# Issuing the first weight load and the x load in front of the program's opening all-engine barrier

## The chip, the cores and the metric

The kernel runs on one core of a Trainium2 chip, with nothing on the other cores. The metric is the device time of one execution in microseconds (us), as the median of several runs. A profile of one execution goes with each kernel; its "span" runs from the first to the last instruction of the program and is some 1.2 us shorter than the device time.

## The reference, cut to what matters

One decode step of two branches that share a layer norm of `x` (1024 values): attention over a cache of 65536 positions, and a small mixer with an MLP.

```python
xn = layernorm(x)                                    # 1 x 1024
q  = xn @ wq                                         # wq 1024 x 4096: 8.4 MB
o  = softmax(q k^T / sqrt(128)) v                    # k_cache, v_cache: 4 x 65536 x 128 each, 67 MB each
A  = o @ wo                                          # wo 4096 x 1024: 8.4 MB
B  = mixer and MLP of layernorm(xn) with w1, w2 (2.1 MB each), w3, w4 (7.3 MB each)
out = x + A + B
```

All is in bf16. There is one row of activations, so every weight and every cache element is read once and used little: about 170 MB go through the core for one row of output.

## The kernel before

The program is written engine by engine. Each engine has a list of operations and waits; at the end the lists are emitted. An engine's DMA issue is an ordinary entry in its list: the transfers of the weights and of the cache are issued by SP (SyncE), the load of `x` by ScalarE.

```python
def _dma(q, chan, fn, reads=(), writes=(), partial=False):
    _deps(q, reads, writes)              # waits for the buffer's readers and writers
    chan.n += 1
    ev = q.dma(fn, chan.sem, 16 * chan.n)
    ...
# the first loads: x on ScalarE's queue, 4 MB + 4 MB of wq and the first K and V blocks (4 MB each) on SP's
_dma(q_act, chan("x"), lambda e: e.dma_start(out=x_bf[:, :], in_=A_x[0, 0, :].rearrange("(p j) -> p j", p=P)), writes=[b_x])
load_rows(Kn[:, 1, :], b_K[1], "wqa", A_wq, 0, 4)
load_rows(Vn[:, 1, :], b_V[1], "wqb", A_wq, 4, 4)
...
issue_k(0)
issue_v(0)
# GpSimd: 12 memsets and 11 selects that build constants, then waits
...
# layer norm of x (DVE, PE, POOL), projection of q in two halves (wqa, then wqb), then
issue_k(1)                               # the buffer of wqa is free again
issue_v(1)                               # the buffer of wqb is free again
# 32 steps, 2 per K/V block; K and V have two buffers each; weights of the other branch go in between
...
q_sp.emit(nc.sync); q_act.emit(nc.scalar); q_pool.emit(nc.gpsimd); q_dve.emit(nc.vector); q_pe.emit(nc.tensor)
...
nc = _bacc.Bacc("TRN2", ...)             # this line (L653) emits a preamble: four constants written by
                                         # GpSimd, then a barrier of all engines, before anything above
```

The barrier of the preamble works so: every other engine executes a drain that counts up one semaphore; GpSimd runs a drain of its own, waits for the full count, then counts up a second semaphore that the others wait for. The semaphores named in the trace records of these instructions show this.

Of the kernel before, what the change touches and what calls it, by code (L numbers as in the profile page):

```python
# [123 lines left out]
def bass_parallel_sum__gqa_block_cached__mixer_s_mlp__decode_kernel(  # L124
# [30 lines left out]
    with ExitStack() as es:  # L155
# [476 lines left out]
        ev_out = _dma(q_sp, chan("out"), lambda e: e.dma_start(out=out[0, 0, :].rearrange("(j n) -> j n", j=4), in_=orow[0:97:32, :]), reads=[b_orow])  # L632
        q_sp.wait(ev_out)

        q_sp.emit(nc.sync)
        q_act.emit(nc.scalar)
        q_pool.emit(nc.gpsimd)
        q_dve.emit(nc.vector)
        q_pe.emit(nc.tensor)
# [28 lines left out]
```

## Time and profile before

The kernel before takes 403.08 us (403.03 to 403.28, 4 runs), with a span of 401.7 us.

| what | value | where to read it |
|---|---|---|
| busy share of VectorE, the busiest compute engine | 57% | first part of the page |
| mean busy share of the 16 DMA engines from 30 to 390 us | 1.00, at 432 GB/s | busy time by stretches |
| first load issued | 0.79 us | timeline |
| first packet of it starts | 1.83 us | packet records of the trace |
| last compute | 399.50 + 0.42 us | timeline |

These are lines of the page of the kernel before: busy time by engine, the rates in 40 slices, and the chain that ended last.

```profile
PE 186.4 (46%) x1859; PEld 78.5 (20%) x1875; DVE 228.4 (57%) x401; ACT 48.9 (12%) x128; POOL 61.8 (15%) x90
...
DMA  8999999999999999999999999999999999999994
GB/s 359 424 418 438 445 418 424 460 419 421 436 447 419 429 435 435 422 436 445 420 428 450 426 419 441 441 419 428 434 439 421 447 432 424 426 425 436 437 416 207
...
DMA 55%; DVE 24%; PE 16%; issue 2%; ACT 1%; SPq 0%; another core or an unknown queue 0%; POOL 0%; ACTq 0%
```

The busy time by stretches of the same kernel; the last two columns are the mean busy share of the DMA engines and what they moved.

```profile
30.00:390.00 360.00, 173.14 (x1664) 72.01 (x1680) 220.52 (x365) 47.03 (x126) 55.91 (x62) 0.55 1.00 432
390.00:402.00 12.00, 5.65 (x112) 2.91 (x112) 0.42 (x1) 0.00 (x0) 0.00 (x0) 0.64 0.54 228
```

The reader is to see two things. First, no compute engine is near its limit, while the DMA row is full in every slice but the first and the last. Second, the chain puts only 55% on the transfers and 24% on VectorE, which looks like a mixed bound. It is not one. A link of the chain such as "VectorE frees the K buffer, then the load of the next K block" begins at the issue of that load; but at its issue the queue still holds earlier loads. The page gives 27.3 us from issue to landing (the median of 15) for a K block of 4 MB that needs about 10 us of the stream by itself (4.19 MB at 432 GB/s). The packet records say it directly: between 2.75 and 395.1 us 15 to 19 data packets are in flight, 16.02 on average, which is one for each DMA engine.

So the run is a sum of three terms: the start of the stream (1.8 us to the first packet), 170.2 MB at 432 GB/s (394 us), and a tail, which is the remaining 5.9 us of the span. The change works on the first term. Here are lines of the timeline of the opening, and the last cast (start in us, duration in us, engine, line, operation).

```profile
0.79 0.40 ACTq L275 DMA_DIRECT2D x_bf<-in_A_x_dram  x1
...
0.79 0.40 SPq L272 DMA_DIRECT2D Kn<-in_A_wq_dram  x1
...
1.25 0.41 SPq L272 DMA_DIRECT2D Vn<-in_A_wq_dram  x1
...
13.05 0.17 DVE L326 CAST xT<-x_bf 128x8 f32<-128x8 bf16 x1 [11.60 <-DMA x_bf<-in_A_x_dram]
...
17.88 0.62 PE L376 MATMUL PT_ps<-Kn,xn_bf 128*32 128x512 bf16 x4
...
21.42 0.33 SPq L286 DMA_DIRECT2D Kn<-in_A_k_cache_dram  x1
...
399.50 0.42 DVE L631 CAST orow<-OUT_ps 128x256 bf16<-128x256 f32 x1 [12.73 <-PE OUT_ps L404]
```

And these are GpSimd's two steps of the barrier and the preamble's drains, from the view of the line that emits them (count, duration in ns, first and last start in us).

```profile
L653 POOLq EVENT_SEMAPHORE  x2: 17/17/17, 0.6 to 0.7; - x2
L653 SPq DRAIN  x1: 7/7/7, 0.0 to 0.0; - x1
...
L653 ACTq DRAIN  x1: 8/8/8, 0.1 to 0.1; - x1
...
L653 POOLq DRAIN  x1: 172/172/172, 0.4 to 0.4; - x1
```

SP is there at 0.00 us and has nothing to do until the barrier lets it go at 0.71. GpSimd's constants and drain hold the barrier: it begins to collect at 0.59. So the first load is issued only at 0.79 us, and its first packet starts at 1.83 us, although it needs nothing that the barrier protects.

The timeline also shows a second candidate for a gain: `x` is 2 KB and yet the first use waits for it until 13.05 us. Its 128 packets of 16 bytes sit between packets of 32 KB. The Trainium skill ("DMA: Bandwidth & Descriptors", section "Queues, rings and completion order") says that each DMA engine takes turns between its queues a packet at a time. The packet records agree: 16 packets of `x` start per round, as many as there are DMA engines, the first of them at 3.63, 4.84, 6.06 ... 12.14 us, 1.21 us apart, which is the duration of a 32 KB packet. An earlier `x` would start the layer norm and the projection earlier.

### The profile page before, as it was taken

The numbers are of one execution on the slowest core, as the hardware profiler recorded it, in microseconds if no ns is written. First come the engines' busy times: TensorE is split into PE (matmuls) and PEld (weight loads), VectorE is DVE, ScalarE is ACT, GpSimd is POOL, SyncE is SP. The second block draws the span as 40 slices with busy tenths as digits, with TensorE's granted clock in tenths as the row PEclk, the third lists the DMA queues.
The fourth block names the chain that finished last, engine by engine and source line by source line (L and its number), as shares of the span: only waits on it lengthen the run. The fifth ranks groups of instructions, "written<-read, shape, count | busy, mean of one in ns | idle before, by whom it ended". The sixth has DMA issues, their size and how long they took to land.

```text
span 401.7 us, 4776 instructions
## 1 busy us (share of the span) xinstructions
PE 186.4 (46%) x1859; PEld 78.5 (20%) x1875; DVE 228.4 (57%) x401; ACT 48.9 (12%) x128; POOL 61.8 (15%) x90
## 2 busy tenths in 40 slices
PE   0332325064525745285531965353433654444664
PEld 0211101021103511062110731121111311111132
DVE  0247566277816578255744287576836775788410
ACT  1000111011101011011110011111201111112100
POOL 5000003012211011110310101111110112112110
PEclk9985556556565556555655555656555656565566
DMA  8999999999999999999999999999999999999994
GB/s 359 424 418 438 445 418 424 460 419 421 436 447 419 429 435 435 422 436 445 420 428 450 426 419 441 441 419 428 434 439 421 447 432 424 426 425 436 437 416 207
DMA packets 7087, 170.19 MB, mean 424 GB/s; under 512 B 916, under 2 KB 920, under 8 KB 1048
## 3 DMA queue, kind: packets, MB, share of 16 engines
q1 hardware_dynamic: 6920, 169.87, 98.4%
q8 instruction: 15, 0.25, 0.2%
q14 instruction: 8, 0.07, 0.0%
q10 hardware_dynamic: 144, 0.00, 0.0%
HBM read 169.87 MB, written 0.00 MB: 423 GB/s over the span
## 4 chain that ended last, share of the span: by engine, by line
DMA 55%; DVE 24%; PE 16%; issue 2%; ACT 1%; SPq 0%; another core or an unknown queue 0%; POOL 0%; ACTq 0%
DMA Kn<-in_A_k_cache_dram 44%; DVE X L476 13%; DMA Kn<-in_B_w_dram 6%; DMA Vn<-in_A_wq_dram 5%; PE H_ps L366 4%; PE S_ps L488 3%; DVE pT_f L529 3%; PE OT_ps L536 3%; DVE mrow L495 3%; PE M_ps L366 1%; ACT p_sb L518 1%; PE PT_ps L527 1%; PE M_ps L564 1%; PE OUT_ps L404 1%; DVE Yall L393 1%
## 5 line engine op out<-in xcount | busy, mean ns | idle before, releaser
L476 DVE STREAM_TRANSPOSE X<-Kn 128x1024 f32<-128x1024 f32 x128 | 151.7, 1215 | 67.4 <-DMA Kn<-in_A_k_cache_dram 67.4
L536 PE MATMUL OT_ps<-Vn,pT_f 128*32 128x512 bf16 x512 | 60.7, 627 | 52.4 <-DVE pT_f L529 52.4
L488 PE MATMUL S_ps<-X,Yall 128*32 128x512 bf16 x512 | 59.1, 608 | 16.1 <-DVE X L476 16.1
L501 PE MATMUL MB_ps<-Rm,Lmat 128*128 128x16 bf16 x32 | 6.1, 192 | 90.1 <-DVE Rm L496 90.1
L550 POOL TENSOR_TENSOR O_acc<-O_acc,tmpO 128x513 f32<-128x513 f32 x28 | 32.8, 1172 | 88.6 <-ACT tmpO L544 88.6
L518 ACT ACTIVATE p_sb<-S_ps,brun 128x512 bf16<-128x512 f32 x32 | 22.0, 687 | 192.7 <-DVE brun L516 157.3
L548 POOL TENSOR_SCALAR O_acc<-O_acc,ff 128x513 f32<-128x513 f32 x28 | 19.5, 698 | 153.4 <-ACT ff L523 153.4
L495 DVE TENSOR_REDUCE mrow<-S_ps 128x1 f32<-128x512 f32 x32 | 21.6, 674 | 25.5 <-PE S_ps L488 25.5
L544 ACT ACTIVATE tmpO<-OT_ps 128x512 f32<-128x512 f32 x32 | 19.1, 598 | 108.0 <-PE OT_ps L536 108.0
L488 PEld LDWEIGHTS S_ps<-X,Yall 128*32 128x32 bf16 x512 | 16.6, 126 | 54.7 <-DVE X L476 38.2
L529 DVE STREAM_TRANSPOSE pT_f<-PT_ps 128x512 f32<-128x512 f32 x32 | 22.9, 716 | 6.1 <-PE PT_ps L527 4.2
L536 PEld LDWEIGHTS OT_ps<-Vn,pT_f 128*32 128x32 bf16 x512 | 14.6, 129 | 59.2 <-DVE pT_f L529 42.0
L501 PEld LDWEIGHTS MB_ps<-Rm,Lmat 128*128 128x128 bf16 x32 | 3.3, 102 | 114.9 <-DVE Rm L496 114.9
L527 PE MATMUL PT_ps<-p_sb,permR 128*128 128x512 bf16 x16 | 9.3, 580 | 21.4 <-ACT p_sb L518 21.4
L366 PEld LDWEIGHTS H_ps<-xn_bf,W 128*128 128x128 bf16 x224 | 14.4, 169 | 1.7 <-issue 1.7
L366 PE MATMUL H_ps<-xn_bf,W 128*128 128x1 bf16 x224 | 14.5, 202 | 0.0
L527 PEld LDWEIGHTS PT_ps<-p_sb,permR 128*128 128x128 bf16 x32 | 3.4, 105 | 41.4 <-ACT p_sb L518 41.4
L505 DVE TENSOR_REDUCE Bst<-MB_ps 128x1 f32<-128x16 f32 x32 | 5.6, 174 | 8.3 <-PE MB_ps L501 8.3
L330 PE MATMUL M_ps<-ln_s,ones_f 128*128 128x1 f32 x6 | 1.8, 362 | 17.3 <-DVE ln_s L329 17.3
L546 POOL COPY O_acc<-tmpO 128x513 f32<-128x513 f32 x4 | 2.4, 612 | 47.4 <-ACT tmpO L544 47.4
L404 PE MATMUL OUT_ps<-Kn,gh_bf 128*1 128x256 bf16 x112 | 5.6, 364 | 5.0 <-DMA Kn<-in_B_w_dram 5.0
L631 DVE CAST orow<-OUT_ps 128x256 bf16<-128x256 f32 x1 | 0.4, 425 | 12.7 <-PE OUT_ps L404 12.7
(109 smaller groups left out, 116.6 us busy)
## 6 DMA issues: line engine op xcount, KB each, us to landing
Kn<-in_A_k_cache_dram SPq DMA_DIRECT2D x15, 4096.0 KB, 27.3
Vn<-in_A_v_cache_dram SPq DMA_DIRECT2D x15, 4096.0 KB, 23.3
W<-in_B_w_dram SPq DMA_DIRECT2D x2, 3584.0 KB, 24.9
W<-in_A_wo_dram SPq DMA_DIRECT2D x3, 2048.0 KB, 23.8
Kn<-in_A_wq_dram SPq DMA_DIRECT2D x1, 4096.0 KB, 12.1
Vn<-in_A_wq_dram SPq DMA_DIRECT2D x1, 4096.0 KB, 21.2
W<-in_B_w_dram SPq DMA_DIRECT2D x2, 2048.0 KB, 33.8
Kn<-in_A_k_cache_dram SPq DMA_DIRECT2D x2, 2048.0 KB, 25.3
```

Source lines behind the costliest of these rows:

```text
L366: fns.append(lambda e, j=j, cx=cx: e.matmul(ps_tile[:, c0 + cx:c0 + cx + 1], lhs_fn(j - j0, cx), rhs_fn(j), start=(j == 0 and cx == 0), st ...
L404: fns.append(lambda e, lhs=lhs, rhs=rhs, jj=jj: e.matmul(OUT_ps[32 * jj:32 * jj + 1, 0:256], lhs, rhs[:, 256 * jj:256 * jj + 256], start=F ...
L476: _op(q_dve, lambda e, ix=ix: e.transpose(out=X32[:, xs, 1024 * ix:1024 * (ix + 1)], in_=Kn32[:, s, 4096 * half + 1024 * ix:4096 * half + ...
L488: fns.append(lambda e, we=we, cm=cm, mv=mv: e.matmul(S_ps[32 * cm:32 * cm + 32, :], Yall[:, h, we, :, :].rearrange("p a g -> p (a g)"), mv ...
L495: _op(q_dve, lambda e: e.reduce_max(mrow[:, m:m + 1], S_ps[:, :], axis=AX.X), reads=[b_S], writes=[b_mrow[m]])
L518: _op(q_act, lambda e: e.activation(p_sb[:, m, :], S_ps[:, :], ACTF.Exp, bias=brun[:, kn:kn + 1], scale=SCALE, accum_out=tmpO[:, m, 512:513]),
L527: _op(q_pe, lambda e: e.matmul(PT_ps[:, :], permR[:, :], p_sb[:, m, :], start=True, stop=True), reads=[b_p[m], b_const], writes=[b_PT])
L529: _op(q_dve, lambda e: e.transpose(out=pT_f[:, :], in_=PT_ps[:, :]), reads=[b_PT], writes=[b_pT])
L536: fns.append(lambda e, q=q, q4=q4: e.matmul(OT_ps[32 * q4:32 * q4 + 32, :], pT_bf[:, q, :, 1], Vn[:, s, 8192 * half + 512 * q:8192 * half ...
L544: _op(q_act, lambda e: e.activation(tmpO[:, m, 0:512], OT_ps[:, :], ACTF.Copy), reads=[b_OT], writes=[b_tmpO[m]], partial=True)
L548: _op(q_pool, lambda e: e.tensor_scalar(out=O_acc[:, :], in0=O_acc[:, :], scalar1=ff[:, m:m + 1], scalar2=0.0, op0=ALU.mult, op1=ALU.add), ...
L550: _op(q_pool, lambda e: e.tensor_tensor(out=O_acc[:, :], in0=O_acc[:, :], in1=tmpO[:, m, :], op=ALU.add), reads=[b_tmpO[m]], writes=[b_Oacc])
```

## The change

The intent is to let SP issue the first 4 MB load, and ScalarE the load of `x`, while the other engines are still on their way to the barrier. Both transfers write buffers that nobody has used, and whoever reads them waits for their semaphores, so the barrier orders nothing for them. The instructions are the same; two of them are placed ahead of the drain of their engine.

```diff
+        code = nc.m.functions[0].blocks[0].instructions
+        heads = {e: next(i for i in code if i.opcode == "Drain" and i.engine == e) for e in (nc.sync.engine, nc.scalar.engine)}
+        n_before = len(code)
         q_sp.emit(nc.sync)
         q_act.emit(nc.scalar)
+        for eng, n_first in ((nc.sync.engine, 1), (nc.scalar.engine, 1)):
+            first = [i for i in code[n_before:] if i.engine == eng][:n_first]
+            assert all(i.opcode == "DMACopy" and not i.sync_info.on_wait for i in first)
+            for i in first:
+                code.remove(i)
+            at = code.index(heads[eng])
+            code[at:at] = first
         q_pool.emit(nc.gpsimd)
```

## The prediction

> **What bounds the kernel now.** The transfers do. The busy time by stretches shows the 16 DMA engines at share 1.00 and 432 GB/s from 30 to 390 us, against VectorE busy for 220.5 of those 360 us. In the trace's packet records 16 data packets are in flight at every moment from 2.7 to 395.1 us: the stream never runs dry. The chain of waits names cache loads for 44% and VectorE for 24%, but the VectorE pieces only time the issue of a load into a queue that still holds work (4 MB takes 20 to 30 us from issue to landing, and alone needs about 10). So the run is: start of the stream + 170.2 MB at 432 GB/s (394 us) + a tail of a few us (0.6 us of matmul, 0.42 us cast, the output's transfer, issued at 399.95 and landed at 401.3).
>
> **What the change moves.** Nothing is added or removed. [...] The load's first packet starts at 1.83, 1.03 us after its issue. With the change SP issues at 0.00 to 0.05 and ScalarE at 0.13 to 0.18. The first packet should start near 1.05, and the whole stream 0.75 to 0.79 us earlier. The second load, behind the barrier, is issued near 0.8 instead of 1.25, which matters nothing: it queues behind 4 MB.
>
> SP's drain then comes at about 0.46 and ScalarE's at about 0.6. GpSimd is ready to collect at 0.59, so the barrier may release up to 0.1 us later; only constants and the 1.28 us table load follow it there, off the path.
>
> x will not overtake the load: its 128 packets of 16 bytes alternate one for one with 32 KB packets of 1.21 us on each engine, 8 rounds, which is why 2 KB took 12.2 us. The Trainium skill, "DMA: Bandwidth & Descriptors", section "Queues, rings and completion order", says each DMA engine takes turns between queue rows at packet granularity; the trace agrees. ScalarE still starts 0.13 us after SP, so x should land near 11.7 to 12.3 instead of 13.0, and the first layer norm moves with it.
>
> **How much is on the critical path.** All of the 0.75 to 0.79 us, since nothing between 2.7 and 395 us limits the stream but its own rate, and buffers are released as much earlier. That is 0.19%.
>
> **Prediction.** 403.12 − 0.75 = about 402.4 us, range 401.9 to 403.0 (runs of before scatter by 0.25 us; another chip may add a bit). Faster by over 2%: 0.01; within 2%: 0.98; slower: 0.01.
>
> **What would show the steps right or wrong.** First load issued at 0.0 in the span, first packet near 1.05, x landing near 12.2, second load issued near 0.8 to 0.9; the same 432 GB/s and share 1.00 in the middle; span near 400.9; every K issue of the middle about 0.8 us earlier; the same tail.
>
> **What would make it wrong.** If the first packet waits for something other than its issue (queue set-up packets end 0.07 us before the span), part is lost. If the drain waits for the transfers to land, the barrier opens some 12 us late and everything behind it suffers. If x got ahead of the load, the projection would start earlier without any end-to-end gain, because the stream bounds it.

## More of the kernel before

The tail is more than compute: from 395.2 us on, fewer than 16 packets are in flight, and the last packet of the loads ends at 398.44 us.

## The result, and the profile after

The changed kernel takes 402.18 us (402.10 to 402.22, 4 runs) against 403.08 us (403.03 to 403.28, 4 runs) before: 0.90 us less by the medians, with no overlap of the runs. The ratio is 0.9979, with a 95% interval of 0.9964 to 0.9993, which is a gain of 0.3 to 1.5 us. Ratios here are not quite the ratio of the medians quoted. The span went from 401.66 to 400.95 us.

The opening and the last cast in the timeline after:

```profile
0.00 0.39 SPq L272 DMA_DIRECT2D Kn<-in_A_wq_dram  x1
0.12 0.37 ACTq L275 DMA_DIRECT2D x_bf<-in_A_x_dram  x1
...
0.91 0.33 SPq L272 DMA_DIRECT2D Vn<-in_A_wq_dram  x1
...
12.34 0.17 DVE L326 CAST xT<-x_bf 128x8 f32<-128x8 bf16 x1 [10.76 <-DMA x_bf<-in_A_x_dram]
...
17.16 0.62 PE L376 MATMUL PT_ps<-Kn,xn_bf 128*32 128x512 bf16 x4
...
20.59 0.33 SPq L286 DMA_DIRECT2D Kn<-in_A_k_cache_dram  x1
...
398.80 0.42 DVE L631 CAST orow<-OUT_ps 128x256 bf16<-128x256 f32 x1 [13.00 <-PE OUT_ps L404]
```

The first load is issued at 0.00 instead of 0.79 us, and the lines from the cast of `x` on are 0.70 to 0.83 us earlier. GpSimd's steps and the drains after:

```profile
L663 POOLq EVENT_SEMAPHORE  x2: 17/17/17, 0.7 to 0.8; - x2
...
L663 SPq DRAIN  x1: 115/115/115, 0.5 to 0.5; - x1
L663 ACTq DRAIN  x1: 145/145/145, 0.5 to 0.5; - x1
```

A drain took 7 or 8 ns before and takes 115 and 145 ns behind a DMA issue. It does not wait for the transfer, which lands 12 us after its issue. GpSimd now begins to collect at 0.71 instead of 0.59 us: the barrier opens 0.12 us later. The middle and the tail after:

```profile
30.00:390.00 360.00, 180.35 (x1686) 71.44 (x1690) 220.36 (x365) 47.00 (x126) 55.96 (x62) 0.56 1.00 431
390.00:402.00 12.00, 6.32 (x112) 2.93 (x100) 0.42 (x1) 0.00 (x0) 0.00 (x0) 0.50 0.47 197
```

The middle is unchanged: share 1.00, 431 GB/s, the same busy time of VectorE. (The difference in PE's busy time and count is of records missing from a trace, not of work.) In the last stretch the DMA share is lower because the same stream ends earlier in a fixed window. The last packet of the loads ends at 397.75 instead of 398.44 us, and the last cast starts at 398.80 instead of 399.50 us.

### The profile page after: what moved, and what is told of

Its sections match the earlier page's. It is cut to its first block, busy times and chain, and to the rows that moved or that the text cites. A ratio compares the mean times of both kernels' runs of the same rounds, so it can differ in the third digit from the quotient of the medians.

```text
span 400.9 us, 4792 instructions
## 1 busy us (share of the span) xinstructions
PE 194.8 (49%) x1875; PEld 78.5 (20%) x1875; DVE 228.3 (57%) x401; ACT 48.9 (12%) x128; POOL 61.8 (15%) x90
## 4 chain that ended last, share of the span: by engine, by line
DMA 55%; DVE 23%; PE 17%; ACT 2%; issue 2%; POOL 0%; SPq 0%; ACTq 0%
DMA Kn<-in_A_k_cache_dram 44%; DVE X L476 12%; DMA Kn<-in_B_w_dram 6%; DMA Vn<-in_A_wq_dram 5%; PE H_ps L366 4%; PE S_ps L488 3%; DVE pT_f L529 3%; PE OT_ps L536 3%; DVE mrow L495 3%; ACT p_sb L518 2%; PE PT_ps L527 2%; PE M_ps L366 1%; PE M_ps L564 1%; PE OUT_ps L404 1%; DVE Yall L393 1%
## 5 line engine op out<-in xcount | busy, mean ns | idle before, releaser
L527 PE MATMUL PT_ps<-p_sb,permR 128*128 128x512 bf16 x32 | 17.5, 548 | 38.6 <-ACT p_sb L518 38.6
L404 PE MATMUL OUT_ps<-Kn,gh_bf 128*1 128x256 bf16 x112 | 6.7, 413 | 4.3 <-DMA Kn<-in_B_w_dram 4.3
```

What stands on the lines that cost most here:

```text
L404: fns.append(lambda e, lhs=lhs, rhs=rhs, jj=jj: e.matmul(OUT_ps[32 * jj:32 * jj + 1, 0:256], lhs, rhs[:, 256 * jj:256 * jj + 256], start=F ...
L527: _op(q_pe, lambda e: e.matmul(PT_ps[:, :], permR[:, :], p_sb[:, m, :], start=True, stop=True), reads=[b_p[m], b_const], writes=[b_PT])
```

## The experiments

There are three theories of where 0.8 us came from.

- Theory S: the transfer stream is the only bound; the time moves one for one with the start of the first load.
- Rival X: the gain comes from `x`, which lets the layer norm and the projection start earlier.
- Rival B: the opening of the barrier matters by itself. If so, its delay of 0.12 us has eaten part of the gain, and more loads in front of it would hurt.

A fourth, Rival V, questions the ground under S: VectorE or the chain of waits bounds the middle, and the transfers only follow.

Nine kernels were run. The first four shared one chip and nine runs of the kernel before (403.04 us, 402.72 to 403.23); the next four shared another and seven runs of the kernel before (402.99 us, 402.82 to 403.21); the last had a chip of its own, with nine runs of the kernel before (402.93 us, 402.83 to 403.31). All gave correct results.

### e1_both: the changed kernel as the yardstick

The edit is the change itself.

> The changed kernel again, as the yardstick for the three beside it on the same chip. Theory S (the transfer stream is the only bound, so the time moves one for one with the first load's start): about 0.8 us under the kernel before (0.75 to 0.95), first packet of the load near 1.0 us, barrier released near 0.8. Rival X (the gain comes from x and the first layer norm starting earlier): the same number, so this run alone separates nothing.

Measured: 402.24 us (402.00 to 402.43), ratio 0.9980 (0.9966 to 0.9993). The gain is there again on another allotment: 0.80 us by the medians.

### e2_load_only: the weight load alone

```diff
-        for eng, n_first in ((nc.sync.engine, 1), (nc.scalar.engine, 1)):
+        for eng, n_first in ((nc.sync.engine, 1),):
```

> Only the 4 MB load goes in front of the barrier; x stays behind it. Theory S: the whole gain stays, within 0.1 us of the run with both moved; x is issued near 0.8 and still lands near 11.8, because its 8 packets per ring take turns with the load's, whose rounds now start earlier. Rival X: the gain is gone or mostly gone, time within 0.2 us of the kernel before.

Measured: 402.28 us (402.07 to 402.42), ratio 0.9981 (0.9968 to 0.9993). The whole gain stays: it differs from the yardstick by 0.04 us, far less than the scatter of either kernel, as S says.

```profile
0.00 0.39 SPq L272 DMA_DIRECT2D Kn<-in_A_wq_dram  x1
...
0.79 0.38 ACTq L275 DMA_DIRECT2D x_bf<-in_A_x_dram  x1
...
14.63 0.17 DVE L326 CAST xT<-x_bf 128x8 f32<-128x8 bf16 x1 [13.16 <-DMA x_bf<-in_A_x_dram]
```

One expectation was missed: `x` landed at 14.6 us, not 11.8. In this timeline its first use is at 14.63 us, 1.6 us later than in the kernel before, and still the kernel gains its 0.76 us. That makes the case against Rival X stronger than planned: the chain that starts with `x` became later and the time did not care. The packet records show why the guess was off: issued 0.79 us after the load, `x` gets its first packet at 5.30 us, only after three packets of the load on each DMA engine, where an `x` issued together with the load came after one. Barrier and constants are where they were before (GpSimd collects at 0.59), so it was ScalarE's issue that held the barrier by 0.12 us in the changed kernel.

### e3_x_only: the x load alone

```diff
-        for eng, n_first in ((nc.sync.engine, 1), (nc.scalar.engine, 1)):
+        for eng, n_first in ((nc.scalar.engine, 1),):
```

> Only x goes in front of the barrier. x is then about 0.7 us ahead of the load, so its tiny packets find idle rings and land near 1.5 to 3 us instead of 12.5; the first layer norm then waits for the constants at about 6.5 us and ends near 10, and the first half of the projection starts when its weights land, near 13, against 17.9 before: 4 to 5 us earlier. ScalarE's drain holds the barrier by about 0.1 us. Theory S: all that buys nothing at the end; time 0 to 0.2 us ABOVE the kernel before (the load starts about 0.1 later). Rival X: faster by 0.8 us or more, up to 4.

Measured: 403.05 us (402.96 to 403.17), ratio 1.0001 (0.9988 to 1.0013).

```profile
0.12 0.38 ACTq L275 DMA_DIRECT2D x_bf<-in_A_x_dram  x1
...
0.93 0.39 SPq L272 DMA_DIRECT2D Kn<-in_A_wq_dram  x1
...
1.92 0.48 DVE L326 CAST xT<-x_bf 128x8 f32<-128x8 bf16 x1 [0.32 <-DMA x_bf<-in_A_x_dram]
...
13.08 0.62 PE L376 MATMUL PT_ps<-Kn,xn_bf 128*32 128x512 bf16 x4 [2.10 <-DMA Kn<-in_A_wq_dram]
...
16.80 0.33 SPq L286 DMA_DIRECT2D Kn<-in_A_k_cache_dram  x1
...
22.75 0.62 PE L376 MATMUL PT_ps<-Vn,xn_bf 128*32 128x512 bf16 x4 [6.07 <-DMA Vn<-in_A_wq_dram]
```

Here `x` lands 11 us earlier, the first half of the projection starts 4.8 us earlier, and the next K block is issued 4.6 us earlier; and the time is that of the kernel before. The lines show where the head start goes: the second half of the projection waits 6.07 us for its weights, which come when the stream brings them, and the early issue of the K block only joins a queue. Rival X falls.

### e4_four_loads: all four opening loads of SP

```diff
-        for eng, n_first in ((nc.sync.engine, 1), (nc.scalar.engine, 1)):
+        for eng, n_first in ((nc.sync.engine, 4), (nc.scalar.engine, 1)):
```

> All four opening loads of the SP queue go in front of the barrier. SP's drain then comes after about 2 us of issue, the barrier opens near 2.3 instead of 0.8 and GpSimd's constants end near 8 instead of 6.4, still before x lands near 11.8. Theory S: the same time as with one load moved, within 0.15 us. Rival B (the opening of the barrier matters to somebody on the path): about 1.5 us slower than the run with one load moved.

Measured: 402.18 us (402.07 to 402.49), ratio 0.9980 (0.9967 to 0.9992). The last drain is SP's now, and the barrier opens late:

```profile
L663 SPq DRAIN  x1: 125/125/125, 2.1 to 2.1; - x1
L663 SPq EVENT_SEMAPHORE  x1: 17/17/17, 2.4 to 2.4; - x1
```

The engines leave the barrier at 2.4 us instead of 0.8 and the time is the yardstick's within 0.06 us. So Rival B falls, too: up to 1.6 us of barrier delay cost nothing that these runs resolve. The reason fits the timeline: VectorE waits for `x` until 12.48 us, long after the barrier. Nor do more early issues help: one load of 4 MB keeps the DMA engines busy for about 10 us, so the second has time.

### e5_x_late: x held back, in the kernel before

```diff
+        q_act.wait((q_pool.sem, 23))       # after GpSimd's last constant
         _dma(q_act, chan("x"), ...)
```

> The kernel before, with x issued only after GpSimd's last constant (about 6.3 us instead of 0.8). x then lands near 17 to 18 instead of 13, the layer norm and the projection's first half move 4 to 5 us later, and the third cache load of K is issued about 3 to 5 us later than 21.4, still long before the 16.8 MB in front of it have landed (about 40 us). Theory S: no change, within 0.2 us of the kernel before. Rival X (this chain is on the path): 4 to 5 us slower.

Measured: 402.86 us (402.77 to 403.16), ratio 0.9996 (0.9980 to 1.0013). The delay came out larger than expected, because `x`, issued at 6.29 us, found its first turn only at 9.96 us.

```profile
6.29 0.37 ACTq L276 DMA_DIRECT2D x_bf<-in_A_x_dram  x1
...
20.36 0.17 DVE L327 CAST xT<-x_bf 128x8 f32<-128x8 bf16 x1 [18.89 <-DMA x_bf<-in_A_x_dram]
...
25.18 0.62 PE L377 MATMUL PT_ps<-Kn,xn_bf 128*32 128x512 bf16 x4
...
28.73 0.33 SPq L287 DMA_DIRECT2D Kn<-in_A_k_cache_dram  x1
```

The chain of `x`, layer norm, projection and next issue is 7.3 us later than in the kernel before (28.73 against 21.42 us for the same K issue), and the time did not move. The SP timelines tell where the 7.3 us were absorbed: the next K issue is 6.2 us late (52.41 against 46.17), the V issue after it only 0.25 us (60.27 against 60.02). Later issues stay 0.3 to 0.5 us late, and the final cast 0.28; the profiled run was the slowest of the four (403.16 us), so these last tenths are not read further. The four opening loads, 16.8 MB, feed the stream until about 40 us (an estimate: 39 us at 432 GB/s after a start at 1.8). The next K issue, at 21.42 us in the kernel before, could therefore come up to some 18 us later before the stream ran dry.

### e6_load_late_12 and e7_load_late_23: the first load held back, in the kernel before

```diff
+        q_sp.wait((q_pool.sem, 12))        # e6: after GpSimd's twelfth memset; e7: 23, its last constant
         load_rows(Kn[:, 1, :], b_K[1], "wqa", A_wq, 0, 4)
```

> The kernel before, with the first load (and so the whole SP queue) held until GpSimd's twelfth memset, near 2.5 us instead of 0.79: 1.75 us later. x goes ahead of it and lands near 2 to 3 us. Theory S: 1.6 to 1.9 us slower than the kernel before, one for one. Rival (there is slack in the stream that the double buffering takes up): under 0.8 us slower.

> The same with the first load held until GpSimd's last constant, near 6.3 us: 5.5 us later than in the kernel before. Theory S: 5.3 to 5.7 us slower, so that with the held-by-1.75 run and the moved run four starts lie on one line of slope 1. Rival (slack): clearly under 5 us.

Measured: e6 404.64 us (404.18 to 404.73), ratio 1.0039 (1.0024 to 1.0054); e7 408.31 us (408.15 to 408.37), ratio 1.0132 (1.0116 to 1.0147). The first load in the timelines of e6 and of e7:

```profile
2.50 0.39 SPq L272 DMA_DIRECT2D Kn<-in_A_wq_dram  x1
...
6.29 0.39 SPq L272 DMA_DIRECT2D Kn<-in_A_wq_dram  x1
```

This is the dose to set beside the change (time against the kernel before of the same chip, by the medians):

| kernel | first load issued at | moved by | first packet of it | `x` first used at | time moved by |
|---|---|---|---|---|---|
| before | 0.79 | | 1.83 | 13.05 | |
| after | 0.00 | −0.79 | 1.02 | 12.34 | −0.90 |
| e1, both | 0.00 | −0.79 | 1.03 | 12.35 | −0.80 |
| e2, load alone | 0.00 | −0.79 | 1.02 | 14.63 | −0.76 |
| e4, four loads | 0.00 | −0.79 | 1.02 | 12.48 | −0.86 |
| e3, `x` alone | 0.93 | +0.14 | 1.95 | 1.92 | +0.01 |
| e5, `x` late | 0.80 | +0.01 | 1.81 | 20.36 | −0.13 |
| e6, load late | 2.50 | +1.71 | 3.52 | 2.44 | +1.65 |
| e7, load later | 6.29 | +5.50 | 7.30 | 2.44 | +5.32 |

The third column predicts the last within 0.2 us over a range of 6.3 us, and the fifth column does not predict it at all. This is Theory S with slope 1 (5.32 / 5.50 = 0.97 at the far end). The three runs in which `x` was out of the way of the load (e3, e6, e7) lie 0.06 to 0.18 us below the slope, but so does e5 where it was not; this is the scatter of the runs and not read further.

### e8_w2_half: fewer bytes, the same arithmetic

```diff
-            load_rows(W[:, 0:8192], [b_W], "w", B_w2, 0, 8)
+            load_rows(W[:, 0:4096], [b_W], "w", B_w2, 0, 4)
```

> The kernel before with half of the second weight matrix left unloaded (1.05 MB of 170.2 MB; wrong result on purpose, all arithmetic kept). Theory S: 1.05 MB at 432 GB/s, 2.4 us faster (2.2 to 2.7). Rival V (VectorE or the chain of waits bounds the middle, and the transfers only follow): under 1 us faster.

Measured: 400.53 us (400.31 to 400.70), ratio 0.9939 (0.9924 to 0.9954): 2.46 us less by the medians, where 1.05 MB at 432 GB/s make 2.43. The busy time by stretches has the same compute in the middle as before, 220.63 us of VectorE against 220.52, and the same full stream:

```profile
30.00:390.00 360.00, 185.07 (x1720) 74.05 (x1724) 220.63 (x365) 47.06 (x126) 56.17 (x62) 0.55 1.00 431
```

Rival V falls: with the arithmetic kept, leaving bytes out gives their full share of the stream's time. (e7 speaks against it as well: a middle with slack would have taken up part of its 5.50 us.)

The result, expected to be wrong, was correct. The mixer shifts its rows by one or two positions and pads; with one position in the sequence only padding is left, so the product with `w2` is zero whatever `w2` holds. The kernel indeed multiplies `w2` by a vector that GpSimd set to zero, and never reads what it computes with `w1`. That points to a version with fewer bytes.

### e9_no_w1_w2: the changed kernel without the two weights that the answer does not depend on

The edit, with the two VectorE lines shortened:

```diff
         def w2_pe():
-            mm_cols(M1_ps, 272, KT_D, lambda j, cx: W[:, j * D + cx:(j + 1) * D:8], lambda j: g_bf[:, j:j + 1], 0, 8, 8, [b_W, b_const], b_M1)
-            _op(q_dve, ... x1 = xn + M1_ps ...)
-            _op(q_dve, ... acc = acc + M1_ps ...)
+            _op(q_dve, lambda e: e.tensor_copy(x1[:], xn[:]), reads=[b_xn], writes=[b_x1])
             out_resid()
...
-        w_seq = [(0, w1_dma, 3, w1_pe), (4, w2_dma, 7, w2_pe),
+        w_seq = [(4, lambda: None, 7, w2_pe),
```

> The changed kernel without the loads of w1 and w2 and without the matmuls and the GELU on them. With one position in the sequence every shifted part of the mixer is padding, so the reference's product with w2 is zero whatever w1 and w2 hold (for finite weights), and the kernel before multiplies w2 by a vector of zeros and never reads the result of w1; the answer stays right. 4.19 MB of 170.2 MB leave the stream. Theory S: 4.19 MB at 432 GB/s, 9.7 us under the changed kernel, so about 392.5 us (392.0 to 393.2), if the two buffers each of K and V keep the stream full without those loads; in the packet records 16 packets stay in flight from about 1.5 to 385 us. Rival V (VectorE or the waits bound the middle): VectorE loses only about 4 us of work at most, so under 4 us of gain, and the DMA share in the middle falls clearly under 1.00.

Measured: 392.39 us (392.23 to 392.77), ratio 0.9740 (0.9727 to 0.9753) to the kernel before, 10.54 us less by the medians. Of these about 0.8 are the early start (e1), which leaves 9.7 for 4.19 MB, as 432 GB/s make it. The stream stays full, at the same rate, beside VectorE work that hardly changed:

```profile
30.00:380.00 350.00, 166.62 (x1542) 66.02 (x1562) 219.50 (x358) 46.82 (x125) 55.96 (x62) 0.56 1.00 431
```

In the packet records 15 to 19 data packets, 16.02 on average, are in flight from 1.8 to 384.5 us, as in the kernel before. This version beats both kernels, but it is a different kind of step: it is right only for a sequence of one position and for finite weights, and it leaves out reads and arithmetic that the answer does not need, where the change only moves an issue. It was run for what the bytes are worth.

As far as placing instructions goes, the experiments point to nothing better: the first load is issued by the first instruction of the span, and neither more early loads nor an early `x` add to it.

## Why the prediction was right, point by point

- The bound. It was read as the transfer stream, against a chain of waits that named VectorE for 24%. e8 and e9 confirm it with 2.46 and about 9.7 us for bytes worth 2.43 and 9.7 us, e7 with 5.32 us for a start 5.50 us later.
- The size. 402.4 us were predicted, in a range of 401.9 to 403.0; measured were 402.18 and, again, 402.24 us. The start moved by 0.79 us, the top of the predicted 0.75 to 0.79; the time by 0.90 and 0.80. The remaining tenth is not explained. It is within the scatter of runs (0.1 to 0.5 us within a kernel), and the two profiled spans differ by only 0.71 us. The stated range alone proves little: it allowed for any gain from about 0.1 to 1.2 us. What bears the account is that the time followed the first load in the experiments.
- The origin. The first load was issued at 0.00 us, its first packet started at 1.02 us (1.05 predicted), so the start of a transfer is not held by something else than its issue.
- `x`. It did not overtake the load and moved with it: it landed at 12.3 us and was first used at 12.34, against a landing at "11.7 to 12.3" predicted. The chain behind it was said to be without value at the end, which e3 (first half of the projection 4.8 us earlier) and e5 (7.3 us later) both show.
- The barrier. "Up to 0.1 us later" was too small: it was 0.12 us, because the drains behind an issue took 115 and 145 ns instead of 7 and 8. That cost nothing; e4 delays the barrier by 1.6 us at no cost.
- A step that was too strict: "every K issue of the middle about 0.8 us earlier". Most were 0.55 to 0.92 us earlier, but the one at 337.96 us moved by 0.10 only, and in e1 one of them was even 1.19 us later, near 46 us. Issues have slack of several microseconds (e5), so a single one says little; the last cast, 0.70 us earlier, is the better mark.

The weight load alone makes the gain (e2). The half of the change that moves `x` does nothing for the time (e3).

## What to carry to other kernels

When the DMA engines are full from the first load to the last, the run is the start of the stream plus bytes over rate plus a tail, and a start that comes earlier by d is worth d, here within 0.2 us over starts from 0.8 us earlier to 5.5 us later; any load that needs nothing from the opening barrier can be issued in front of it, and one is enough if it lasts longer than the barrier (here 10 us against 0.8). A chain of waits that passes through an issue into a queue that still holds work does not show a bound: look whether the queue ever runs dry, and test the chain by delaying it, since a wait can be added without a race. And where bytes over rate is the large term, ask of every byte whether the answer depends on it.

## What the Trainium skill lacked or had wrong

- "DMA: Bandwidth & Descriptors", section "Queues, rings and completion order": turns are taken packet by packet, and the records agree once both queues are served. The page does not say how late a newcomer gets its first turn. Issued within 0.12 us of the load, `x` came after one 32 KB packet of it on each DMA engine; issued 0.79 us after it (e2), after three; issued at 6.29 us into a running stream (e5), its first packet came 3.67 us later. On idle DMA engines (e3) the load of `x` had its first packet 1.0 us after issue, so about 2.7 us of the 3.67 were spent behind other packets, a little over two of 1.21 us. That each DMA engine has some two packets committed behind the one it is moving is an inference from these.
- The same page, section "Latency and other measured facts": about 600 ns to the first byte for a DMA issued by SP or ScalarE. The page does not say from where it counts. Here the first packet of the first load started 1.01 to 1.04 us after the start of the issuing instruction and 0.62 to 0.64 us after its end, in every kernel, moved or not. Counted from the end, the figure agrees; counted from the start, the 0.39 us of the instruction itself come on top.
- The same page, section "Where 436 GB/s comes from": it says that for transfers between HBM and SBUF the HBM side, about 358 GB/s (half of a stack's 716, which two cores share), binds. With one core running alone this stream held 431 to 432 GB/s for 350 to 360 us, near the 435 that the page gives as the ceiling of the fabric; the page's own 425 GB/s for 16 MB, which it says is a single-core figure, fits better.
- "VectorE: DVE Perf Modes", section "The DRAIN you can't avoid": the drains that the runtime puts around a kernel are put at a constant of about 12 ns. The section does not speak of the drains that a program's own opening barrier has (L653 and L663 here). These took 7 to 10 ns where nothing stood before them, but 111 to 145 ns on SP and ScalarE right behind a DMA issue, and 172 to 174 ns on GpSimd behind its memsets.
- No page that was read here says that a load can be issued in front of the program's opening barrier, nor what it is worth: 0.76 to 0.90 us in four comparisons. "DMA: Bandwidth & Descriptors", section "Issuing engines are not separate DMA queues", says that issuing from several engines saves only the sequencer's issue time. No run here tests that, since `x` was issued by ScalarE in every kernel.
